# Gate/up remainders of three PSUM tiles behind one change to row tiles, in a fused attention and gated-MLP kernel

## The chip, the cores and the metric

The kernel runs on one NeuronCore of a Trainium2 chip. The metric is the device time of one execution in microseconds (us). Engines are named as in the profile: PE is TensorE's matmul side, PEld its weight loads, DVE is VectorE, ACT is ScalarE, POOL is GpSimd, SP is the SyncE queue that issues most DMAs.

## What is computed

One adaLN-conditioned transformer block on x of 2048 rows by 576 columns, in bf16. Attention is local and dilated (window 8, dilation 2, 32 heads of 18). The MLP is gated without a nonlinearity. Cut to what matters:

```python
mod = (silu(c) @ w_mod)                      # six rows of 576: sa, ca, ga, sb, cb, gb
h = layernorm(x) * (1 + ca) + sa
x = x + ga * attention(h, wqkv, wo)
h = layernorm(x) * (1 + cb) + sb
g = h @ w_gate                               # 576 -> 4608
u = h @ w_up                                 # 576 -> 4608
x = x + gb * ((g * u) @ w_down)              # 4608 -> 576
```

## The kernel before

**Tiling.** The 4608 hidden columns are 36 FF tiles of 128. The contraction over 576 is four full tiles of 128 rows and a remainder of 64. In `gate_up` a "main" step does the four full tiles for one FF tile, for gate (t=0) and up (t=1): 8 matmuls with 128 by 128 weights. The "remainder" does the last 64 rows. The gate's 64 weight rows lie in partitions 0 to 63 and the up's in 64 to 127 of one tile (`gr`), and the 64 remaining rows of h2T are held in both halves, so the two remainder matmuls use the two halves of the array's rows ("row tiles") and run side by side. One FF tile is thus 8 main matmuls and one pair of remainders.

**Passes.** The 2048 rows are cut into ten chunks (`SIZES`: four of 128, six of 256). Seven passes run gate/up: passes 0 to 3 on 128 rows each (the short passes, one chunk), passes 4 to 6 on 512 rows (the long passes, two chunks). After passes 3, 4, 5 and 6 a `down` stage multiplies the 512 rows gathered so far with w_down (L661). Each pass takes the FF tiles in nine blocks of four (`FB`), in an order that differs by pass (`ORDER`).

**Weights.** The main weights of a block (`gm`, 1 MB) and its remainder rows (`gr`, 128 KB) go through a ring of three buffers. Blocks 2 to 5 are kept during passes 0 to 3 in the place of w_down (so their matmuls show `wd` as input). `block_done` issues the next block's load, or in pass 3 the load of a part of w_down into a kept block's place; such a DMA starts once TensorE has read the old contents for the last time. All of these go through SP in the order in which they are written.

**PSUM.** `ps_mlp` has three tiles of two banks each, used by gate/up and by down; `ps_att` has two banks for the attention. A gate/up tile holds gate and up of one FF tile with 512 rows, or of two FF tiles with 128 rows. When it is complete, ScalarE copies it out as bf16 into one of two `gu` buffers (L644) and VectorE multiplies gate by up into `hh` (L645). These evacuations are traced under high priority.

**Order.** While a pass runs, the attention of the next pass's chunks is woven in: `project` makes q, k, v (L444, L451, L469); `attend` makes the logits (L512, with 32-column tiles of the array), the softmax, the weighted sum, the projection with wo (L583), the second layernorm and the transposes (L398) that give h2T for the next pass. They are generators. `step(ns)` in `gate_up` and `down` advances a Pacer's clock by so many ns of matmul time, and where the clock has come to the next part's share of the pass (`AT`, `AT_SHORT`; 0.60 for wo0, 0.80 for h2T in the short passes), the Pacer emits that part, one for each step. In passes 0 to 3 the framework's planner orders every engine by priority and by when it thinks that inputs are ready; in passes 4 to 6 TensorE runs in the order written, and the other engines are planned.

**Groups.** Remainders are gathered: in a short pass the two PSUM tiles of a block get their main matmuls and then their 8 remainders together; in a long pass two PSUM tiles are followed by their 4 remainders, twice in each block.

Of the kernel before, what the change touches and what calls it, by code (L numbers as in the profile page):

```python
# [7 lines left out]
BF = mybir.dt.bfloat16  # L8
F32 = mybir.dt.float32
ALU = mybir.AluOpType  # L10
# [7 lines left out]
P = 128  # L18
D = 576
DP = 640  # L20
KT = 5
# [10 lines left out]
CM = 512  # L32
# [4 lines left out]
FB = 4  # L37
AUTO = 4
GU_BUFS = 3
NB = FT // FB  # L40

ORDER = [[0, 1, 2, 3, 4, 5, 6, 7, 8], [6, 7, 8, 5, 4, 3, 2, 1, 0], [8, 1, 0, 5, 4, 3, 2, 6, 7],
         [2, 3, 4, 5, 0, 6, 7, 1, 8], [7, 1, 8, 0, 2, 3, 4, 5, 6], [4, 5, 6, 0, 1, 2, 3, 7, 8],
         [3, 7, 8, 0, 1, 2, 4, 5, 6]]
# [15 lines left out]
def kernel(  # L60
# [13 lines left out]
    nc = tc.nc  # L74
# [7 lines left out]
    def pool(name, bufs, **kw):  # L82
        return ctx.enter_context(tc.tile_pool(name=name, bufs=bufs, **kw))
# [13 lines left out]
    ps_mlp = pool("ps_mlp", 3, space=PSUM)  # L97
# [4 lines left out]
    def hp():  # L102
        return tc.high_priority()
# [11 lines left out]
    for sl, m0, off in ((slice(0, KT), 0, 0), (slice(KT, KT + 1), KT - 1, -64)):  # L115
        n = sl.stop - sl.start
# [132 lines left out]
    rows = {}  # L249
# [20 lines left out]
    gu_blocks = {}  # L270
# [45 lines left out]
    def load_next(ts=(0, 1)):  # L316
        if state["next"] < len(loads):
            load_gu(loads[state["next"]], ts)
            state["next"] += 1

    def load_wd(f0, f1):
        nc.sync.dma_start(wd[:, f0:f1, :], B_w_down[f0 * P:f1 * P, :].rearrange("(k p) n -> p k n", p=P))

    def block_done(pi, b):
        if pi == KEPT_PASSES - 1 and b in KEPT:
            k = KEPT.index(b)
            load_wd(k * WDB, (k + 1) * WDB)
        for n in range(len(loads)):
            if last_use[n] == (pi, b) and n + GU_BUFS == state["next"]:
                load_next()  # L330
# [16 lines left out]
    late = {}  # L347
# [246 lines left out]
    def gate_up(pi, c0, C, h2, step):  # L594

        hh = late["hh"]
        cs = slice(c0, c0 + C)  # L600
        ns = C / 2.4

        def main(out, gm, i, first):
            for t in range(2):
                for kt in range(KT - 1):
                    nc.tensor.matmul(out(t), lhsT=gm[:, kt, t, i * P:(i + 1) * P], rhs=h2[:, kt, cs],  # L606
                                     start=(kt == 0 and first), stop=False, skip_group_check=True)

        def rem(outs, gr, i):
            for hf in range(2):  # L610
                for t in range(2):
                    rows = slice(64 * t, 64 * (t + 1))
                    nc.tensor.matmul(outs[hf](t), lhsT=gr[rows, (i + 2 * hf) * P:(i + 2 * hf + 1) * P],  # L613
                                     rhs=h2[rows, KT - 1, cs], start=False, stop=True, skip_group_check=True)

        for b in ORDER[pi]:
            gm, gr = gu_blocks[b]
            todo = []
            for i in range(FB // 2):
                if C <= 256:  # L620

                    ps = ps_mlp.tile([P, 2, 2, 256], F32, name="pgu", tag="mlp")
                    outs = [lambda t, ps=ps, hf=hf: ps[:, t, hf, 0:C] for hf in range(2)]
                    evac = [(ps[:, :, :, 0:C].rearrange("p t n c -> p n t c"), slice(b * FB + i, b * FB + i + 3, 2))]
                else:
                    pss = [ps_mlp.tile([P, 2, 512], F32, name="pgu", tag="mlp") for _ in range(2)]
                    outs = [lambda t, ps=ps: ps[:, t, 0:C] for ps in pss]
                    evac = [(pss[hf][:, None, :, 0:C], slice(b * FB + i + 2 * hf, b * FB + i + 2 * hf + 1)) for hf in range(2)]
                todo.append((outs, i, evac))
                for hf in range(2):  # L630
                    main(outs[hf], gm, i + 2 * hf, hf == 0 or C > 256)
                    if hf == 0 or (C <= 256 and i == 0):
                        step(8 * ns)
                if C <= 256 and i == 0:
                    continue
                for outs, i, evac in todo:
                    rem(outs, gr, i)
                with hp():
                    for _, _, evac in todo:
                        for src, fs in evac:  # L640
                            n = src.shape[1]
                            gu = late["gup"].tile([P, 2 * CM], BF, name="gu")
                            g = gu[:].rearrange("p (n t c) -> p n t c", n=n, t=2)[:, :, :, 0:C]
                            nc.scalar.copy(g, src)  # L644
                            nc.vector.tensor_tensor(hh[:, fs, cs], g[:, :, 0, :], g[:, :, 1, :], ALU.mult)  # L645
                todo = []
                if i == FB // 2 - 1:
                    block_done(pi, b)
                step(10 * ns)

    def down(di, r0, x_t, step):
        to_load = [(cx, j) for cx in LOAD_X_DOWN.get(di, []) for j in range(SIZES[cx] // P)]
# [110 lines left out]
    def run_pass(pi):  # L763
        di, p = passes[pi]
        last = p is DOWN[di][-1]
        C = sum(SIZES[c] for c in p)
        total = FT * 9 * C / 2.4 + (FT * CM // P * 240 if last else 0)
        step = Pacer(passes[pi + 1][1] if pi + 1 < len(passes) else [], total)
        step(0)
        gate_up(pi, home[p[0]][1], C, h2T[di], step)  # L770
        if last:
            r0 = START[DOWN[di][0][0]]
            down(di, r0, [t for q in DOWN[di] for c in q for t in x_tiles[c]], step)
        step(0, rest=True)
# [36 lines left out]
```

## Time and profile before

| what | value |
|---|---|
| runs, median (lowest to highest) | 597.45 us (596.89 to 598.4), 4 runs |
| profiled execution | 596.89 us, span 595.1 us |
| granted TensorE clock | 1.0 |
| passes 0 to 3 with their attention | 38.7 to 161.8 us of the span |
| pass 4, pass 5, pass 6 (gate/up) | 216.2 to 306.9, 353.0 to 441.2, 481.0 to 553.8 us |
| casts of one gate/up tile on ScalarE | 587 ns (short), 1013 ns (long) |
| HBM read, written | 70.93 MB, 4.74 MB |

Between the passes lie the down stages. In the profile a group is named by its line, its engine and operation, and output<-inputs with their shapes; "x" counts instructions. In a timeline the first number is the start in us from the span's start, the second the duration of the merged piece. Ends of matmuls are modelled, so distances between starts say more than durations.

### The profile page before, as it was taken

The page shows a single profiled execution, that of the slowest core. Times are in us where ns is not written, and L with a number is a line of the kernel's source. Part 1 is how long each engine was busy: PE and PEld are TensorE (multiplying, and loading weights), DVE is VectorE, ACT ScalarE, POOL GpSimd, SP SyncE. Part 2 cuts the span into 40 slices and gives each one's busy share as a digit, 9 for nine tenths or more (in the row PEclk, how much of TensorE's full clock was granted, in tenths as well). Part 3 has the DMA queues.
Part 4 walks back from the last instruction along what each step waited for, and adds up shares of the span by engine and source line. Part 5 has one row for each costly group of instructions (what it writes and reads, how often), then busy time and mean ns, then how long its engine had stood idle before and what let it go on. Part 6 is the DMA issues. An engine that isn't in the chain of part 4 may idle for free.

```text
span 595.1 us, 12426 instructions
## 1 busy us (share of the span) xinstructions
PE 574.8 (97%) x5254; PEld 373.0 (63%) x5289; DVE 317.1 (53%) x705; ACT 261.5 (44%) x462; POOL 59.3 (10%) x117
## 2 busy tenths in 40 slices
PE   6879999999999999999999999999999999999996
PEld 3649798888878864544358874544458753433675
DVE  4767676767868766636385245834464422212101
ACT  3336667666552355456551145555540134444200
POOL 3530101010111200010001200011000000000000
PEclk9999999999999999999999999999999999999999
DMA  9999753459641333357000502456200004440000
GB/s 279 286 341 343 249 161 107 146 180 308 203 155 36 112 108 123 117 178 237 4 1 30 189 21 80 142 171 196 70 1 11 21 24 146 160 159 1 1 21 20
DMA packets 55073, 76.47 MB, mean 128 GB/s; under 512 B 3690, under 2 KB 48378, under 8 KB 55018
## 3 DMA queue, kind: packets, MB, share of 16 engines
q1 hardware_dynamic: 44922, 44.88, 24.4%
q0 software_dynamic: 7200, 27.48, 13.9%
q10 hardware_dynamic: 2896, 3.32, 1.6%
q8 instruction: 41, 0.67, 0.5%
q14 instruction: 14, 0.11, 0.1%
HBM read 70.93 MB, written 4.74 MB: 127 GB/s over the span
## 4 chain that ended last, share of the span: by engine, by line
PE 84%; DMA 6%; ACT 4%; DVE 4%; issue 1%; POOL 1%; ACTq 0%; SPq 0%; POOLq 0%; DVEq 0%
PE pgu L606 39%; PE acc L661 22%; PE pgu L613 6%; PE pq L444 5%; DMA wm<-in_w_mod_dram 3%; PE lgT L512 2%; PE pvA L469 2%; PE pvB L469 2%; DMA gm<-in_B_w_up_dram 1%; DMA wqk<-in_A_wqkv_dram 1%; PE pwB L583 1%; PE pwA L583 1%; PE turnA L398 1%; ACT gu L644 1%; ACT xn L377 1%
## 5 line engine op out<-in xcount | busy, mean ns | idle before, releaser
L606 PE MATMUL pgu<-h2T,gm 128*128 128x512 bf16 (+1 forms) x1473 | 238.1, 310 | 4.2 <-DMA wd<-in_B_w_gate_dram 1.5
L644 ACT CAST gu<-pgu 128x1024 bf16<-128x1024 f32 (+1 forms) x180 | 142.5, 844 | 137.1 <-PE pgu L613 127.4
L606 PEld LDWEIGHTS <-gm 128*128 128x128 bf16 x1504 | 117.7, 98 | 107.2 <-issue 17.6
L661 PE MATMUL acc<-wd,hh 128*128 128x288 bf16 x1152 | 147.4, 286 | 0.6 <-DVE y L667 0.6
L645 DVE TENSOR_TENSOR hh<-gu 128x512 bf16<-128x512 bf16 (+1 forms) x180 | 65.2, 368 | 145.8 <-ACT gu L644 145.0
L661 PEld LDWEIGHTS <-hh 128*128 128x128 bf16 x1152 | 111.8, 98 | 29.9 <-issue 2.4
L503 DVE TENSOR_TENSOR prod<-qT,kT 128x1280 bf16<-128x1280 bf16 (+1 forms) x80 | 46.3, 631 | 6.0 <-PE lgT L512 4.2
L613 PE MATMUL pgu<-h2T,gr 64*128 64x512 bf16 (+1 forms) x376 | 41.7, 312 | 0.9
L444 PE MATMUL pq<-hT,wqk 128*128 128x256 bf16 (+1 forms) x400 | 40.9, 251 | 1.6 <-DVE hT L408 1.6
L667 DVE TENSOR_TENSOR y<-acc,gb_bc 128x576 bf16<-128x576 f32 (+1 forms) x17 | 12.2, 715 | 54.3 <-PE acc L661 54.3
L570 DVE TENSOR_TENSOR vsh<-vsh,attn 128x2304 bf16<-128x2304 bf16 x30 | 39.8, 1350 | 0.7 <-DMA vsh<-vd 0.6
L486 POOL DMA_DIRECT2D vsh<-vd x30 | 22.4, 752 | 167.5 <-DMA vd<-v_sb 139.8
L444 PEld LDWEIGHTS <-wqk 128*128 128x128 bf16 x400 | 31.8, 98 | 8.9 <-issue 3.3
L606 PE MATMUL pgu<-h2T,wd 128*128 128x128 bf16 x512 | 34.2, 219 | 0.2 <-ACT gu L644 0.2
L670 POOL DMA_DIRECT2D out_dram<-y x15 | 8.2, 550 | 250.9 <-DVE y L669 239.4
L606 PEld LDWEIGHTS <-wd 128*128 128x128 bf16 x512 | 30.3, 98 | 1.4 <-issue 0.8
L377 ACT ACTIVATE xn<-x_t,ln_nmr,ln_rstd 128x576 bf16<-128x576 bf16 x31 | 26.2, 864 | 6.0 <-DVE ln_nmr L375 4.1
L613 PEld LDWEIGHTS <-gr 64*128 64x128 bf16 x376 | 10.9, 94 | 25.5 <-issue 21.2
L363 DVE BATCH_NORM_STATS2 ln_stats<-x_t 128x6 f32<-128x288 bf16 x64 | 26.0, 446 | 0.8
L446 ACT CAST kT<-pq 128x512 bf16<-128x512 f32 (+1 forms) x18 | 9.2, 519 | 26.0 <-PE pq L444 18.9
L571 DVE TENSOR_TENSOR vsh<-vsh 128x2304 bf16<-128x2304 bf16 x15 | 20.3, 1350 | 0.1
L367 ACT ACTIVATE ln_rstd<-ln_rstd 128x2 f32<-128x2 f32 (+1 forms) x20 | 4.1, 205 | 36.7 <-DVE ln_rstd L366 36.5
(132 smaller groups left out, 472.7 us busy)
## 6 DMA issues: line engine op xcount, KB each, us to landing
vsh<-vd POOLq DMA_DIRECT2D x30, 576.0 KB, 5.9
gm<-in_B_w_gate_dram SPq DMA_DIRECT2D x29, 512.0 KB, 3.7
gm<-in_B_w_up_dram SPq DMA_DIRECT2D x27, 512.0 KB, 5.2
wd<-in_B_w_down_dram SPq DMA_DIRECT2D x4, 1152.0 KB, 7.0
out_dram<-y POOLq DMA_DIRECT2D x15, 144.0 KB, 2.0
wd<-in_B_w_gate_dram SPq DMA_DIRECT2D x4, 512.0 KB, 18.1
wd<-in_B_w_up_dram POOLq DMA_DIRECT2D x4, 512.0 KB, 13.0
gr<-in_B_w_gate_dram SPq DMA_DIRECT2D x29, 64.0 KB, 4.9
```

Source lines behind the costliest of these rows:

```text
L363: nc.vector.bn_stats(stats[:, j, hf, :], src[j][:, hf * 288:(hf + 1) * 288])
L377: nc.scalar.activation(xn[:, j0 + j, 0:D], src[j][:], ACTF.Identity, bias=nmr[:, j:j + 1], scale=rstd[:, j:j + 1])
L444: nc.tensor.matmul(pq[:, gi, 0:C], lhsT=wqk[:, kt, w0:w0 + P], rhs=h[:, kt, :], start=(kt == 0), stop=(kt == KT - 1))
L469: nc.tensor.matmul(pv[q][:, 0:288], lhsT=h[:, kt, j * P:(j + 1) * P], rhs=wv[:, kt, q * 288:(q + 1) * 288], start=(kt == 0), stop=(kt == K ...
L486: nc.gpsimd.dma_start(vsh[:].rearrange("p w d h -> p w (d h)"), src)
L503: nc.vector.tensor_tensor(prod[:, 0:nm, 0:C], qT[:, 0:nm, 0:C], kT[:, 0:nm, off:off + C], ALU.mult)
L570: nc.vector.tensor_tensor(vsh[:], vsh[:], attn[:, j, ws, None, :].to_broadcast([P, WG, DH, H]), ALU.mult)
L606: nc.tensor.matmul(out(t), lhsT=gm[:, kt, t, i * P:(i + 1) * P], rhs=h2[:, kt, cs], start=(kt == 0 and first), stop=False, skip_group_chec ...
L613: nc.tensor.matmul(outs[hf](t), lhsT=gr[rows, (i + 2 * hf) * P:(i + 2 * hf + 1) * P], rhs=h2[rows, KT - 1, cs], start=False, stop=True, sk ...
L644: nc.scalar.copy(g, src)
L645: nc.vector.tensor_tensor(hh[:, fs, cs], g[:, :, 0, :], g[:, :, 1, :], ALU.mult)
L661: nc.tensor.matmul(acc[:, q, 0:288], lhsT=hh[:, f, j * P:(j + 1) * P], rhs=wd[:, f, q * 288:(q + 1) * 288], start=(f == 0), stop=(f == FT ...
```

## The change

Tiles are now numbered through the whole pass ("units": two neighbouring FF tiles in a short pass, one in a long pass) and taken three at a time. Main of the first and of the second; then the remainders of all three, which close the first two tiles and open the third; then a step of the Pacer, the evacuations of the first two, main of the third, which closes it, and its evacuation. `block_done` is called after the group in which a block ended. In a short pass `step` now follows each main; before, the second main of a block's last tile had none. The steps' times add up to 54 units of C/2.4 ns for six FF tiles in every pass; before it was 34 for the four FF tiles of a block in a short pass and 36 in a long one.

```diff
-        def main(out, gm, i, first):
-            for t in range(2):
-                for kt in range(KT - 1):
-                    nc.tensor.matmul(out(t), lhsT=gm[:, kt, t, i * P:(i + 1) * P], rhs=h2[:, kt, cs],
-                                     start=(kt == 0 and first), stop=False, skip_group_check=True)
-
-        def rem(outs, gr, i):
-            for hf in range(2):
...
-        for b in ORDER[pi]:
-            gm, gr = gu_blocks[b]
-            todo = []
-            for i in range(FB // 2):
...
-                todo.append((outs, i, evac))
-                for hf in range(2):
-                    main(outs[hf], gm, i + 2 * hf, hf == 0 or C > 256)
-                    if hf == 0 or (C <= 256 and i == 0):
-                        step(8 * ns)
-                if C <= 256 and i == 0:
-                    continue
-                for outs, i, evac in todo:
-                    rem(outs, gr, i)
-                with hp():
...
-                            nc.scalar.copy(g, src)
-                            nc.vector.tensor_tensor(hh[:, fs, cs], g[:, :, 0, :], g[:, :, 1, :], ALU.mult)
-                todo = []
-                if i == FB // 2 - 1:
-                    block_done(pi, b)
-                step(10 * ns)
+        nf = 2 if C <= 256 else 1
+        units = [(b, i) for b in ORDER[pi] for i in range(0, FB, nf)]
+
+        def main(u, first):
+            (b, i), out = units[u], ps[u]
+            for n in range(nf):
+                for t in range(2):
+                    for kt in range(KT - 1):
+                        nc.tensor.matmul(out[:, t, n, 0:C], lhsT=gu_blocks[b][0][:, kt, t, (i + n) * P:(i + n + 1) * P], rhs=h2[:, kt, cs],
+                                         start=(first and n == 0 and kt == 0), stop=(not first and kt == KT - 2), skip_group_check=True)
+                step(8 * ns)
+
+        def rem(u, first):
...
+                    nc.tensor.matmul(out[:, t, n, 0:C], lhsT=gu_blocks[b][1][rows, (i + n) * P:(i + n + 1) * P], rhs=h2[rows, KT - 1, cs],
+                                     start=(first and n == 0), stop=not first, skip_group_check=True)
+
+        def evacuate(u):
...
+                nc.scalar.copy(g, ps[u][:, :, :, 0:C].rearrange("p t n c -> p n t c"))
+                nc.vector.tensor_tensor(hh[:, fs, cs], g[:, :, 0, :], g[:, :, 1, :], ALU.mult)
+
+        ps, done = {}, 0
+        for u in range(0, len(units), 3):
+            for k in range(3):
+                ps[u + k] = ps_mlp.tile([P, 2, nf, 512 // nf], F32, name="pgu", tag="mlp")
+                if k < 2:
+                    main(u + k, True)
+            for k in range(3):
+                rem(u + k, k == 2)
+            step(6 * nf * ns / 2)
+            evacuate(u)
+            evacuate(u + 1)
+            main(u + 2, False)
+            evacuate(u + 2)
+            while done < NB and (done + 1) * FB <= (u + 3) * nf:
+                block_done(pi, ORDER[pi][done])
+                done += 1
```

More of the change, by code (lines that the diff above doesn't have):

```diff
@@ new lines, in main @@
+        def main(u, first):
[7 more added lines that the diff above has]
+        def rem(u, first):
+            (b, i), out = units[u], ps[u]
+            for n in range(nf):
@@ L611, in rem @@
                 for t in range(2):
                     rows = slice(64 * t, 64 * (t + 1))
-                    nc.tensor.matmul(outs[hf](t), lhsT=gr[rows, (i + 2 * hf) * P:(i + 2 * hf + 1) * P],
-                                     rhs=h2[rows, KT - 1, cs], start=False, stop=True, skip_group_check=True)
-        for b in ORDER[pi]:
-            gm, gr = gu_blocks[b]
-            todo = []
-            for i in range(FB // 2):
[L620 to L628, printed above, removed]
-                todo.append((outs, i, evac))
-                for hf in range(2):
-                    main(outs[hf], gm, i + 2 * hf, hf == 0 or C > 256)
-                    if hf == 0 or (C <= 256 and i == 0):
-                        step(8 * ns)
-                if C <= 256 and i == 0:
-                    continue
-                for outs, i, evac in todo:
-                    rem(outs, gr, i)
-                with hp():
[L639 to L643, printed above, removed]
-                            nc.scalar.copy(g, src)
-                            nc.vector.tensor_tensor(hh[:, fs, cs], g[:, :, 0, :], g[:, :, 1, :], ALU.mult)
-                todo = []
-                if i == FB // 2 - 1:
-                    block_done(pi, b)
-                step(10 * ns)
@@ new lines, in rem @@
+                    nc.tensor.matmul(out[:, t, n, 0:C], lhsT=gu_blocks[b][1][rows, (i + n) * P:(i + n + 1) * P], rhs=h2[rows, KT - 1, cs],
+                                     start=(first and n == 0), stop=not first, skip_group_check=True)
+        def evacuate(u):
+            b, i = units[u]
+            fs = slice(b * FB + i, b * FB + i + nf)
+            with hp():
+                g = late["gup"].tile([P, 2 * CM], BF, name="gu")[:, 0:2 * nf * C].rearrange("p (n t c) -> p n t c", n=nf, t=2)
+                nc.scalar.copy(g, ps[u][:, :, :, 0:C].rearrange("p t n c -> p n t c"))
+                nc.vector.tensor_tensor(hh[:, fs, cs], g[:, :, 0, :], g[:, :, 1, :], ALU.mult)
```

## The prediction

> **What bounds the kernel now.** I read the page's busy times first, then its slices.
>
> ```profile
> span 595.1 us, 12426 instructions
> PE 574.8 (97%) x5254; PEld 373.0 (63%) x5289; DVE 317.1 (53%) x705; ACT 261.5 (44%) x462; POOL 59.3 (10%) x117
> ...
> PE   6879999999999999999999999999999999999996
> ```
>
> TensorE is busy for 97% of the span, and after the first three slices hardly rests; no other engine passes 53%. The granted clock is full in every slice. So time is gained only where TensorE does less or waits less. A busy TensorE is not one at its peak, so I looked next at how its matmuls follow each other, in the timeline of TensorE in the last long pass, which no attention work interrupts:
>
> ```profile
> 485.20 3.63 PE L606 MATMUL pgu<-h2T,gm 128*128 128x512 bf16 x16
> 488.76 0.60 PE L613 MATMUL pgu<-h2T,gr 64*128 64x512 bf16 x4
> 489.29 3.63 PE L606 MATMUL pgu<-h2T,gm 128*128 128x512 bf16 x15
> ```
>
> and in the chain that ended last, which gives the bare rates:
>
> ```profile
> 123.79 1.79 PE pgu L606 x32
> ...
> 233.08 1.73 PE pgu L606 x8
> ```
>
> 1.73/8 is 0.216 us for a 512-column matmul, 1.79/32 is 0.056 us for a 128-column one. From 485.20 to 489.29 one period of the long pass takes 4.09 us. It holds 16 main matmuls and two pairs of remainders, whose halves (64 rows each) start 3 to 4 ns apart: 18 slots of 0.216, 3.89 us. Some 0.20 us are left. The start times show where: from the last main matmul to the first remainder 311 ns, from the last remainder to the next main matmul 308 ns, against 216. That is 95 ns to change to row tiles and 92 ns to change back. With 128 columns the same two distances are 152 and 148 against 56: the same price, so it doesn't scale with the matmul. A round trip costs 0.187 us, and nothing covers it, since TensorE itself stands.
>
> The third reading is the TensorE timeline at the end of the first short pass, which shows what else holds it:
>
> ```profile
> 62.12 1.95 PE L606 MATMUL pgu<-h2T,gm 128*128 128x128 bf16 x32
> 64.00 0.40 PE L613 MATMUL pgu<-h2T,gr 64*128 64x128 bf16 x8
> 64.33 0.40 PE L606 MATMUL pgu<-h2T,gm 128*128 128x128 bf16 x4
> 65.51 1.74 PE L606 MATMUL pgu<-h2T,gm 128*128 128x128 bf16 x28 [0.79 <-DMA gm<-in_B_w_up_dram]
> 67.18 0.23 PE L613 MATMUL pgu<-h2T,gr 64*128 64x128 bf16 x2
> 67.34 0.34 PE L398 MATMUL turnA<-identw,xn 128*128 128x128 bf16 x3
> ...
> 68.86 1.74 PE L606 MATMUL pgu<-h2T,gm 128*128 128x128 bf16 x28 [0.25 <-DMA gm<-in_B_w_up_dram]
> ```
>
> Two things. Blocks 7 and 8 wait for their weights, so the end of pass 0 is pinned to an arrival (the chain has the same transfer as "60.06 8.75 DMA"). And a transpose of the attention sits inside a remainder group, which makes three round trips of one; passes 1 and 2 show the same at 95.24 and 127.73. The last view is the table of windows in pass 3:
>
> ```profile
> 148.00:152.00 4.00, 4.00 (x64) 3.66 (x62) 4.00 (x6) 1.84 (x5) 0.00 (x0) 1.00 1.09 351
> 152.00:156.00 4.00, 4.00 (x61) 3.62 (x59) 3.97 (x7) 2.34 (x6) 0.00 (x0) 1.00 1.08 309
> ```
>
> The last two columns are DMA share and GB/s. The DMA engines are full from 136 to 156: four loads of w_down (issued at 134.23, 137.23, 140.51, 143.80, each as a kept block is released), then blocks 1 and 8. Block 1's up half lands at 154.74, its remainder rows at 155.13 and 155.32, and TensorE starts block 1 at 155.2. There is no slack.
>
> **The change part by part.** *Fewer changes.* A short pass has 9 remainder groups now and gets 6 (18 tiles of two FF tiles, three to a group); a long pass 18, and gets 12. Four short passes: 36 to 24. Three long: 54 to 36. The count of matmuls stays. Long passes: 18 round trips at 0.187 are 3.37 us, all on the path, because TensorE there waits for nothing (its largest stall in 216 to 554 is 0.57 us, one projection waiting for hT). Short passes: 12 at 0.187 are 2.24 us, 0.56 a pass. Passes 1 and 2 keep theirs: 1.12 us.
>
> *Pass 0.* Its 0.56 us goes into the wait for block 8, whose arrival doesn't move: the DMA engines are full there too (share 1.07 from 40.2 to 64.5), and its issue waits for queue space, not for the release of block 1, which comes one tile (0.9 us) later in the new order. From the gate on, 28 main matmuls were left with 8 remainders; now the same with 12, two slots of 0.056: +0.1 us. Bounds: -0.56 (if arrivals move too) and +1.0 (if block 7's remainder rows, landing at 65.66 and just after, hold the third tile's remainders, which now come before its main).
>
> *Pass 3.* Two edits hurt. The second kept block is released with the second group, one tile later, so the second w_down load issues about 1 us later; the first still flows until about 140, so up to 1 us of transfer time may be lost. And block 1 (tiles 14, 15) needs its remainder rows before the main of tile 14, so at about 154.4 instead of 158.6, while they land at 155.3. After that moment remains what remained before. So the 0.56 us is lost and a little more: I take +0.3, between -0.56 (arrivals move with the pass) and +1.5 (both delays in full). I lean to the lower half because the queue, once full, delivers at the same rate.
>
> *Split groups.* Each transpose inside a group costs two extra round trips, 0.37 us. In the new order the attention is emitted slightly earlier in the pass (a block's paces add to 54 per six FF tiles, where they added to 34 per four), so the transposes fall elsewhere; remainders hold only about a fifth of the pass. In passes 1 and 2 that gives up to 0.75 us; it may also stay as it is. I take half, -0.37.
>
> *The third tile's remainder waits for an empty tile.* This is the added wait. There are three PSUM tiles, and all three are now held at a change. What is queued behind is the rest of TensorE's stream. Two main stages pass between the end of the earlier third tile and this wait: about 3.5 us long, 1.8 us short. The cast that must end by then takes 1013 ns (128x1024) or 587 ns (128x512), and may start 1.73 or 0.9 us after the previous group, behind two casts that by then are all but done. That leaves about 2 us and 0.9 us, more than one attention activation of the row xn (864 ns). The first tile of the next group has one main stage of cover, as now, and the trace shows what that costs: two stalls of about 0.4 us in 36 short blocks. So 0, with an upper bound of 24 waits of 0.1 us, 2.4 us; below nothing, at most 0.8, since those two stalls could go.
>
> The Trainium skill, TensorEngine Tiling (Array Packing), under Restrictions and Gotchas, says that row tiling raises PSUM pressure, and under Performance Considerations that the copy out of PSUM may become the bound. That speaks against holding all three tiles at once. Read at its worst, one cast waited for in each group, it would make 36 x 1.013 + 24 x 0.587 = 50.6 us of loss; by the rows above it is nothing, and no run here shows it yet.
>
> *Weight loads.* In the long passes a block comes free up to one tile later (2 us); its successor is needed two blocks (17 us) after issue and lands in 4 to 7, so this stays hidden at no cost. If that cover were gone, it would be 2 us for each load. The step ahead of the evacuations emits attention work a moment earlier; evacuations keep their priority: nothing.
>
> Sum: -3.37 - 1.12 + 0.1 + 0.3 - 0.37 = -4.46. The profiled execution took 596.89 us (span 595.1 and 1.8 around it), so 592.4; the median of the runs, 597.45, is 0.56 above it, so 593.0.
>
> **The rivals.** *The short passes give nothing* because their planned order splits the larger groups as often as before, or the two pinned passes lose in full: then only the long passes count, 3.37 less about 0.5 to 1.5, giving 594.6 to 595.5. For it: three of the four short passes are split now, two are pinned. Against it: only 3 of the 36 groups are split now.
>
> *Slower: the transposes come too early.* Place: the last attention step of short passes 0 to 2, where the projection with wo ends (91.14 in pass 1) and xn is ready only at 95.9, 4.7 us later, by a chain of VectorE and ScalarE that the change doesn't shorten. Between stand about 4.2 us of gate/up work, and TensorE already stalls about 0.5 us there. If the new order put the transposes right behind wo, each pass would lose up to 4.2 us, some 8 to 12 us in all, less 4.5: 601 to 605. It decides from 1.5 us more per pass, when less than about 2.7 us, five FF tiles at 0.56, is left between. The paces plan 0.2 of 36 tiles, 7.2, so I give it little.
>
> *More than reckoned.* Arrivals move with the passes, the splits and both PSUM stalls go: -5.6 - 0.75 - 0.8, about 590.3.
>
> **How the numbers follow.** Forecast (592 to 594) 0.5; short passes give nothing (594.6 to 595.5, some of it to 596.2) 0.26; more than reckoned 0.08; slower 0.10; and 0.06 for savings that small waits eat up wholly. A measurement here can tell about 0.2% (1.2 us) from no change: faster 0.84, same 0.06, slower 0.10. The range, 590.8 to 596.5, leaves out the slower case and the far end of the best.
>
> **What would show it.** Right: in the last pass a period of three FF tiles takes 6.0 us (27 slots and one round trip) with x6 at L613's place and 60 changes in all where unsplit; pass 6's gate/up shortens by 1.1 to 1.2 us; passes 0 and 3 end no earlier, relative to their starts; TensorE waits for remainder rows (gr) in pass 3. Wrong: if a change costs more with six or twelve remainders behind it, if ScalarE's cast ends TensorE's waits in most groups, or if a short pass grows by over 1 us.

## The result and the profile after

The changed kernel takes 597.79 us (median of 37 runs) against 597.76 us for the kernel before (59 runs): a ratio of 1.0003, interval 0.9994 to 1.0012. That is no change, where 593.0 was forecast. The profiled execution took 597.87 us, span 596.1.

The page after, first its span, busy times and TensorE's slices:

```profile
span 596.1 us, 12425 instructions
PE 570.1 (96%) x5254; PEld 376.6 (63%) x5289; DVE 318.0 (53%) x705; ACT 263.5 (44%) x462; POOL 60.7 (10%) x117
...
PE   6878899999999999999999999999999999999996
```

TensorE is busy for 4.7 us less and the span is no shorter: the work went, and idle time came. The timeline of TensorE in the last pass shows that the work went as planned:

```profile
487.62 5.35 PE L612 MATMUL pgu<-h2T,gm 128*128 128x512 bf16 x24
492.90 0.82 PE L621 MATMUL pgu<-h2T,gr 64*128 64x512 bf16 x6
493.66 5.35 PE L612 MATMUL pgu<-h2T,gm 128*128 128x512 bf16 x23
```

One period of three FF tiles takes 6.04 us, 27 slots of 0.216 and 0.21 for one round trip. In the whole trace TensorE changes its tiling 176 times against 248 before. 60 of the 72 are the 30 round trips; the other 12 are the transposes that no longer split a group.

The idle time shows in the table of waits (engine and line, who it waited for, us in total, times, longest), here TensorE's own waits from 38 to 222 us, which covers the short passes and the first down stage. Before:

```profile
PE pgu L606 <- DMA wd<-in_B_w_gate_dram: 1.5, 1, 1.5
PE pgu L606 <- DMA gm<-in_B_w_up_dram: 1.0, 2, 0.8
PE turnA L398 <- ACT xn L377: 0.9, 2, 0.4
PE pgu L606 <- ACT gu L644: 0.5, 2, 0.2
```

and after:

```profile
PE pvB L469 <- ACT kT L454: 3.2, 3, 2.5
PE turnA L398 <- ACT xn L377: 2.0, 3, 0.7
PE pgu L612 <- DVE h2T L408: 1.5, 1, 1.5
PE pgu L621 <- DMA gr<-in_B_w_gate_dram: 1.5, 1, 1.5
PE turnB L398 <- ACT xn L379: 0.7, 3, 0.2
PE turnB L398 <- DVE dd L532: 0.4, 2, 0.2
```

A wait of 1.5 us for the first matmul of pass 0 is in both tables, at L606 before and at L612 after. Before, 2.4 us of other waits are left; after, 7.8 us in these lines and 0.7 in smaller ones. By stage, from the start of the first main weight load of each pass (us; the forecast of -0.37 for the splits is shared between passes 1 and 2):

| stage | before | after | difference | forecast |
|---|---|---|---|---|
| start of pass 0 | 38.66 | 39.08 | +0.4 | 0 |
| pass 0 | 32.19 | 34.91 | +2.7 | +0.1 |
| pass 1 | 28.14 | 28.71 | +0.6 | -0.75 |
| pass 2 | 32.49 | 32.58 | +0.1 | -0.75 |
| pass 3 and down | 84.71 | 86.58 | +1.9 | +0.3 |
| from pass 4 to the end | 378.92 | 374.21 | -4.7 | -3.37 |

Three new waits carry the short passes' loss. **The first** is in passes 0 to 2, at the v projection. TensorE's timeline in pass 0:

```profile
57.90 0.40 PE L469 MATMUL pvA<-wv,hT 128*128 128x288 bf16 x2 [0.16 <-ACT kT L446]
60.82 0.41 PE L469 MATMUL pvB<-wv,hT 128*128 128x288 bf16 x2 [2.52 <-ACT kT L454]
```

pvB needs an attention bank that ScalarE's copy L454 empties. The copy takes 0.26 us, so what matters is what it stands behind. ScalarE's timeline:

```profile
56.98 0.58 ACT L629 CAST gu<-pgu 128x512 bf16<-128x512 f32 x1 [1.13 <-DVE hh L630]
57.47 0.38 ACT L446 CAST kT<-pq 128x256 bf16<-128x256 f32 x1
59.74 0.58 ACT L629 CAST gu<-pgu 128x512 bf16<-128x512 f32 x1 [1.90 <-DVE hh L630]
60.22 0.26 ACT L452 CAST qT<-pr 64x128 bf16<-64x128 f32 x1
60.50 0.26 ACT L454 CAST kT<-pr 64x128 bf16<-64x128 f32 x1
```

It stands behind a gate/up cast that waits 1.90 us for VectorE to free one of the two gu buffers. VectorE's timeline in that time:

```profile
56.81 1.35 DVE L571 TENSOR_TENSOR vsh<-vsh 128x2304 bf16<-128x2304 bf16 x1
58.20 0.76 DVE L572 TENSOR_TENSOR vsh<-vsh 128x1152 bf16<-128x1152 bf16 x1
58.99 0.46 DVE L573 TENSOR_TENSOR o_sb<-vsh 128x576 bf16<-128x576 bf16 x1
59.37 0.48 DVE L630 TENSOR_TENSOR hh<-gu 128x256 bf16<-128x256 bf16 x2
```

The multiplies that free the buffers (L630) stand behind 2.6 us of the attention's weighted sum. In the kernel before, ScalarE came to the same copy (56.76) with nothing of the kind ahead of it, and the next casts waited for no buffer:

```profile
56.48 0.26 ACT L452 CAST qT<-pr 64x128 bf16<-64x128 f32 x1 [0.80 <-PE pr L451]
56.76 0.26 ACT L454 CAST kT<-pr 64x128 bf16<-64x128 f32 x1
57.15 1.07 ACT L644 CAST gu<-pgu 128x512 bf16<-128x512 f32 x2
```

So, as read from these rows, one buffer too few holds ScalarE, ScalarE holds a bank, and the bank holds TensorE. The run with four buffers below tests it.

**The second** is at the transposes near the end of passes 0 to 2, in TensorE's timeline of pass 1:

```profile
98.40 0.34 PE L398 MATMUL turnA<-identw,xn 128*128 128x128 bf16 x3 [0.66 <-ACT xn L377]
...
99.69 0.23 PE L398 MATMUL turnB<-identw,xn 128*128 128x128 bf16 x1 [0.23 <-ACT xn L379]
```

By the start times they hold TensorE for 0.83 and 0.39 us in each of the three passes, where before it was 0.51 in two of them. **The third** is in pass 3, the remainder rows of block 1:

```profile
158.62 0.40 PE L621 MATMUL pgu<-h2T,gr 64*128 64x128 bf16 x8
160.47 0.51 PE L621 MATMUL pgu<-h2T,gr 64*128 64x128 bf16 x4 [1.46 <-DMA gr<-in_B_w_gate_dram]
```

Eight remainders run, and the four that open the third tile wait.

### The profile page after: what moved, and what is told of

It is laid out like the page before. It is cut to its first block, busy times and chain, and to the rows that moved or that the text cites. A ratio compares the mean times of both kernels' runs of the same rounds, so it can differ in the third digit from the quotient of the medians.

```text
span 596.1 us, 12425 instructions
## 1 busy us (share of the span) xinstructions
PE 570.1 (96%) x5254; PEld 376.6 (63%) x5289; DVE 318.0 (53%) x705; ACT 263.5 (44%) x462; POOL 60.7 (10%) x117
## 4 chain that ended last, share of the span: by engine, by line
PE 82%; DMA 6%; DVE 6%; ACT 3%; issue 2%; ACTq 0%; POOL 0%; POOLq 0%; DVEq 0%
PE pgu L612 37%; PE acc L660 23%; PE pgu L621 6%; PE pq L444 5%; DMA vd<-v_sb 3%; PE lgT L512 2%; DMA vsh<-vd 2%; PE pwA L583 1%; PE pwB L583 1%; PE pvB L469 1%; PE pvA L469 1%; ACT gu L629 1%; DMA gr<-in_B_w_gate_dram 1%; PE turnA L398 1%; PE turnB L398 1%
## 5 line engine op out<-in xcount | busy, mean ns | idle before, releaser
L612 PE MATMUL pgu<-h2T,gm 128*128 128x512 bf16 (+1 forms) x1473 | 237.6, 311 | 3.9 <-DVE h2T L408 1.5
L629 ACT CAST gu<-pgu 128x1024 bf16<-128x1024 f32 (+1 forms) x180 | 145.3, 843 | 109.1 <-PE pgu L621 79.8
L612 PEld LDWEIGHTS <-gm 128*128 128x128 bf16 x1504 | 119.2, 98 | 106.1 <-issue 15.5
L630 DVE TENSOR_TENSOR hh<-gu 128x512 bf16<-128x512 bf16 (+1 forms) x180 | 65.6, 368 | 133.7 <-ACT gu L629 132.6
L621 PE MATMUL pgu<-h2T,gr 64*128 64x512 bf16 (+1 forms) x376 | 37.2, 311 | 1.5 <-DMA gr<-in_B_w_gate_dram 1.5
L612 PE MATMUL pgu<-h2T,wd 128*128 128x128 bf16 x512 | 34.0, 219 | 0.0
L612 PEld LDWEIGHTS <-wd 128*128 128x128 bf16 x512 | 30.3, 98 | 1.0 <-issue 0.2
L621 PEld LDWEIGHTS <-gr 64*128 64x128 bf16 x376 | 12.3, 94 | 20.7 <-issue 11.7
L469 PEld LDWEIGHTS <-hT 128*128 128x128 bf16 x160 | 15.2, 98 | 9.0 <-issue 4.9
```

What stands on the lines that cost most here:

```text
L469: nc.tensor.matmul(pv[q][:, 0:288], lhsT=h[:, kt, j * P:(j + 1) * P], rhs=wv[:, kt, q * 288:(q + 1) * 288], start=(kt == 0), stop=(kt == K ...
L612: nc.tensor.matmul(out[:, t, n, 0:C], lhsT=gu_blocks[b][0][:, kt, t, (i + n) * P:(i + n + 1) * P], rhs=h2[:, kt, cs], start=(first and n = ...
L621: nc.tensor.matmul(out[:, t, n, 0:C], lhsT=gu_blocks[b][1][rows, (i + n) * P:(i + n + 1) * P], rhs=h2[rows, KT - 1, cs], start=(first and ...
L629: nc.scalar.copy(g, ps[u][:, :, :, 0:C].rearrange("p t n c -> p n t c"))
```

## The experiments

My theory after the result: the long passes keep what was forecast, and the short passes give theirs back in these three waits. The rivals: a round trip costs less than reckoned, or TensorE's waits are only pushed from place to place, so that taking one away gains nothing.

**New grouping in the long passes alone.** Both versions of `gate_up` stand in the kernel:

```diff
+    def gate_up(pi, c0, C, h2, step):
+        (gate_up_new if C > 256 else gate_up_old)(pi, c0, C, h2, step)
```

> New grouping in the long passes alone, the short ones as before. My theory (the long passes keep their savings, the short ones give theirs back and more in new waits): 18 round trips at 0.187 us and the lost 0.57 us wait, 3.5 to 4.5 us faster than before, about 593.5; the start of pass 4 stays near 216 us of the span. Rival (a change costs less than reckoned, or what is saved comes back as waits in the long passes too): within 1 us of before.

Measured: 593.76 us against 597.59, ratio 0.9941 (0.9927 to 0.9956). Pass 4 starts at 216.45 us, as expected, and from there to the end it takes 374.4 us against 378.9. The long passes' gain is real and stands alone.

**New grouping in the short passes alone.** The same with `C <= 256`.

> New grouping in the short passes alone, the long ones as before. My theory: 2 to 6 us slower than before, with pass 4 starting about 5 us later, as after the whole change. Rival (the short passes' new order costs nothing itself, and the profiled execution after the change only caught an accidental half-clock window): 1 to 3 us faster, as forecast for them.

Measured: 602.8 us, ratio 1.0088 (1.0071 to 1.0104). The short passes lose 5.2 us, and the two halves (-3.8 and +5.2) add up to the whole within 1.4 us. The rival falls as far as it promised a gain. A half-clock window (a stretch of about 3.4 us in which TensorE's granted clock is half; rows in the last section) is in it, though: the profiled execution has a second one at 161.2, and five of the six runs list the same mean granted clock of 0.994. It may make up the 1.4 us that are left over; that is not shown.

**Four gu buffers in the short passes**, each of half the size; the last two lines stand ahead of pass 4.

```diff
-        late["gup"] = pool("gup", 2)
+        late["guard"] = tc.tile_pool(name="gups", bufs=4)
+        late["gup"] = late["guard"].__enter__()
...
-                g = late["gup"].tile([P, 2 * CM], BF, name="gu")[:, 0:2 * nf * C]
+                g = late["gup"].tile([P, CM if C <= 256 else 2 * CM], BF, name="gu")[:, 0:2 * nf * C]
...
+    late["guard"].__exit__(None, None, None)
+    late["gup"] = pool("gup", 2)
```

> The whole change, with four gu buffers of half the size in the short passes instead of two (one tile there needs only half a buffer); nearly the same instruction order on every engine. Theory (the third cast of a group waits for VectorE to free a gu buffer, and ScalarE's copies of q, k, v stand behind it, so TensorE waits for an attention bank at pvB): the waits at pvB in passes 0, 1 and 2 (2.7, 0.7 and 0.3 us) go, 2.5 to 4 us faster than the changed kernel. Rival (TensorE's wait is for the data of the attention, and ScalarE's wait is only its image): less than 1 us.

Measured: 595.63 us, ratio 0.997 (0.9959 to 0.9982), 2.0 us under the kernel before in the same session and 2.2 under the changed kernel's median, somewhat less than expected. The traces have the same order of instructions on every engine, but for one instruction of VectorE that moves by one place; so it is the buffers. TensorE's timeline shows the wait gone at its place in pass 0 (429 ns between the starts of pvA's second and pvB's first matmul, where it was 2.80 us):

```profile
58.33 0.41 PE L470 MATMUL pvA<-wv,hT 128*128 128x288 bf16 x2
58.88 0.41 PE L470 MATMUL pvB<-wv,hT 128*128 128x288 bf16 x2
```

and, later in the same pass, where a part of the gain went:

```profile
66.02 0.40 PE L622 MATMUL pgu<-h2T,gr 64*128 64x128 bf16 x8
67.14 0.48 PE L622 MATMUL pgu<-h2T,gr 64*128 64x128 bf16 x4 [0.72 <-DMA gr<-in_B_w_gate_dram]
```

TensorE now comes to block 7 before its remainder rows do. Before the repair this wait did not show: the longer one came ahead of it.

**The transposes later.**

```diff
-AT_SHORT = dict(AT, oT=.55, wo0=.60, h2T=.80)
+AT_SHORT = dict(AT, oT=.55, wo0=.60, h2T=.88)
```

> The whole change, with the share of the pass at which the last transposes of a short pass are emitted moved from 0.80 to 0.88; they then stand 24 main matmuls (1.3 us) later on TensorE. Theory (they now come ahead of xn, for 0.83 and 0.39 us in each of passes 0 to 2): most of 3.6 us goes, 2 to 3.6 us faster than the changed kernel. Rival (the waits move to the start of the next pass, which then waits for h2T): within 1 us.

Measured: 597.31 us, ratio 0.9988 (0.9972 to 1.0003): by the time the rival, though the waits that came are not for h2T. The waits at the transposes are gone, but in each of passes 0 to 2 a main matmul now waits 0.85 us for a PSUM tile, and at the start of passes 2 and 3 another 0.40 us; both end with ScalarE's cast. The kernel below, which has the same transposes, shows why.

**Pass 3 grouped as before**, the rest changed (`pi != 3` as the condition).

> The whole change, but pass 3 grouped as before. Theory (in pass 3 the third tile's remainders come one main stage before the block's weights would be needed, and the second w_down load is released later; both lie on a full DMA stretch, so TensorE waits 1.6 us for remainder rows): that wait goes, pass 3 and its down stage fall from 86.6 us back to 84.7, and the half-clock window that sometimes follows the wait becomes rare; 2 to 3 us faster than the changed kernel, 595 to 596. Rival (the transfers end when they end, so TensorE waits as long at another place of pass 3): within 0.7 us of the changed kernel.

Measured: 595.79 us, ratio 0.9967 (0.9952 to 0.9981), 2.0 us under the changed kernel's median. Pass 3 and its down stage take 84.52 us, and TensorE no longer waits for remainder rows. So the transfers do arrive in time for the old order. The new order asks for them one main stage earlier and also starts them later (the next section has the times); this run undoes both and does not part them. Half-clock windows became rarer too, as expected: 2 of the 11 runs list a mean granted clock of 0.994 or less, where 20 of the 37 of the changed kernel do.

**Both repairs together**, four gu buffers and 0.88.

> The whole change with both repairs, four gu buffers in the short passes and the transposes at 0.88. If the two waits are separate, the gains add: 2.0 and 0.5 us, so about 595.2, and pass 1 takes 28.0 us. If the wait of 0.85 us that took the transposes' place in the run with 0.88 (a main matmul waiting for ScalarE) was itself for want of gu buffers, it goes too: up to 2.5 us more, 593 to 594. If both repairs ran into the same arrival of weights in pass 0, less than the sum: 595.5 to 596.5.

Measured: 596.17 us, ratio 0.9964 (0.9949 to 0.9979), not better than the buffers alone. Pass 1 takes 27.92 us, as expected. Pass 0 takes 32.97, since TensorE waits 1.78 us for block 7's remainder rows at 64.48 and then 0.74 us for block 8. The third of the expected answers holds: both repairs ran into the same arrivals. With `gate_up` as before in that pass, pass 0 ended at 70.9, 71.1 and 71.2 us in three kernels that entered it at 38.7, 37.5 and 37.9, and at 72.2 in a fourth that entered at 38.9: the first three ends are closer together than their starts, which speaks for an arrival that sets them; the fourth does not fit.

**Mixed**: new grouping in the long passes and in passes 1 and 2, there with both repairs; passes 0 and 3 as before.

```diff
+        (gate_up_new if pi not in (0, 3) else gate_up_old)(pi, c0, C, h2, step)
...
-        at = AT_SHORT if SIZES[ci] == P else AT
+        at = dict(AT_SHORT, h2T=.88) if ci in (2, 3) else AT_SHORT if SIZES[ci] == P else AT
```

> New grouping in the long passes and in passes 1 and 2, there with four gu buffers and the transposes at 0.88; passes 0 and 3, which end on arrivals of weights, as before. Theory: the long passes' gain stays whole, and passes 1 and 2 give a part of their 0.94 us each: 592.5 to 593.5, the fastest of all. Rival (the planned order of any short pass eats what the changes save): not faster than the kernel with new grouping in the long passes alone, 593.8.

Measured: 593.32 us, ratio 0.9922 (0.9908 to 0.9935), faster than both kernels, as expected. The runs do not tell it apart from new grouping in the long passes alone (593.76), so the rival is not ruled out; the traces show passes 1 and 2 shorter by 0.27 and 0.08 us. What takes the rest of their 0.94 us is in TensorE's timeline

```profile
94.90 1.07 PE L670 MATMUL pgu<-h2T,gm 128*128 128x128 bf16 x16
96.65 1.05 PE L670 MATMUL pgu<-h2T,gm 128*128 128x128 bf16 x16 [0.69 <-ACT gu L687]
```

and in ScalarE's:

```profile
94.83 0.20 ACT L369 ACTIVATE ln_rstd<-ln_rstd 128x1 f32<-128x1 f32 x1
95.27 0.87 ACT L378 ACTIVATE xn<-x_t,ln_nmr,ln_rstd 128x576 bf16<-128x576 bf16 x1 [0.23 <-DVE ln_nmr L376]
96.04 1.05 ACT L687 CAST gu<-pgu 128x512 bf16<-128x512 f32 x2
```

The remainders that close two tiles end at 94.9, but their casts stand behind the layernorm's chain on ScalarE until 96.04, and the next tile's main waits for the first of them. The planner had put xn ahead.

**Groups of one in the long passes**: each tile's two remainders follow its main; short passes as before.

```diff
+        for u in range(len(units)):
+            ps[u] = ps_mlp.tile([P, 2, nf, 512 // nf], F32, name="pgu", tag="mlp")
+            main(u, True)
+            rem(u, False)
+            step(2 * nf * ns / 2)
+            evacuate(u)
...
```

> The price of a round trip by itself: short passes as before, and in the long passes each tile's pair of remainders follows its main matmuls, so 108 groups in place of 54 in the three passes. At 0.187 us a round trip, on the path in full: 54 more cost 10.1 us, about 607.7. Rival (a part of the price belongs to a group's weight loads or is hidden by its neighbours, so that it isn't linear in the number of groups): under 605 or over 611.

Measured: 607.9 us, ratio 1.0173 (1.0154 to 1.0193). From pass 4 to the end the trace has 389.2 us, 10.26 more than before for 54 more round trips: 0.190 us each. The timeline of the last pass gives the same, 2.16 us for 9 slots of 0.216 and one trip:

```profile
492.09 1.90 PE L669 MATMUL pgu<-h2T,gm 128*128 128x512 bf16 x8
493.92 0.39 PE L678 MATMUL pgu<-h2T,gr 64*128 64x512 bf16 x2
494.24 1.90 PE L669 MATMUL pgu<-h2T,gm 128*128 128x512 bf16 x8
```

The price is linear in the number of groups, from one pair a group to three.

## Why the prediction was wrong

**The price of a change and the long passes: right.** 0.187 us was read from distances of starts, and the groups of one confirmed it. The term of 3.37 us was small rather than large: 4.5 to 4.7 us in the traces, 3.8 in the medians. The wait of 0.57 us in pass 4 went too; what the rest is, no run settles.

**The added wait of the third tile: the step that failed.** From pass 0 to the first down stage the sum had a gain of 1.1 us, and the traces show a loss of 5.7. The sum put this term at 0, by comparing when the cast "must end" with the stages that TensorE needs. That looked at PSUM tiles and TensorE alone. The wait that came is one resource further: a third cast in a group needs a third gu buffer, there are two, and the one whose turn it is is freed by a multiply behind 2.6 us of attention on VectorE. The step "evacuations keep their priority: nothing" hid this: priority did not put those multiplies ahead of the weighted sum in the order that the planner made. With four buffers about 2 us came back, so about that much is shown for this term; its upper bound was 2.4 us, set for another reason, and the sum took 0. The casts behind xn, of 0.85 us, are the wait that the step did describe, in the form in which it appears once the transposes move.

**The split groups: right in what goes, wrong in what comes.** All 12 changes of the splits went. The rival of transposes that come too early was right in its mechanism and place: TensorE waits 1.2 us at the transposes of each of passes 0 to 2, about 0.7 more than in passes 1 and 2 before. That is under the 1.5 us from which it would have decided by itself. Its price and the gain of -0.37 were kept apart as if only one could happen.

**Pass 3: the mechanism right, the size past the end of its bounds.** The wait for remainder rows is where it was put, and the stage lost 1.9 us where +0.3 was taken and +1.5 was the bound. Going to the lower half was the mistake: block 1's first load was issued 1.3 us later relative to the pass (at 151.86 instead of 146.78, the pass having started 3.8 us later), and its remainder rows were needed earlier as well. It began with the second w_down load, for which about 1 us of delay was reckoned. It was issued at 143.24 instead of 137.23, 2.2 us later relative to the pass.

**Pass 0: pinned, as said, but the new waits reach beyond the pin.** The saving went nowhere, as forecast. The two waits of 2.7 and 1.2 us, and in the profiled execution a half-clock window at 41.7, then carried the pass past the arrival of its weights: the trace of the changed kernel has no wait for them there. How much of the 2.7 us that the pass lost belongs to the window is not shown. The bound of +1.0 did name the remainder rows of block 7; they showed as soon as the wait at pvB was gone.

**The copies out of PSUM.** The Trainium skill, TensorEngine Tiling (Array Packing), Performance Considerations, says that after a fourfold speedup of TensorE the copy out of PSUM may become the bottleneck. The prediction weighed that against rows of cast durations and put it aside. Here the copies do hold TensorE at a few places of the short passes: 3.2 us at pvB in the table of waits, or 0.85 and 0.40 us at a time once the transposes move, and not the 50.6 of the worst reading. They do so because of what they queue behind, not because of how long they take: ScalarE is busy for 44% of the span.

## What to carry to other kernels

A saving on the busiest engine is only worth what the stage around it can take: sum it by stage, and for each stage name the arrival or the buffer that is late next. Where a change makes work come in bursts (three copies instead of two), count every buffer along the way, not the first one alone, and ask on each in-order engine what stands ahead of the instruction that frees it. A stage that is ordered by a planner can change sign with the grouping; undoing the change there alone kept 3.8 us here.

## What the runs showed of the hardware

After some waits TensorE's granted clock falls to half for a window of about 3.4 us. In the kernel with pass 3 grouped as before, the table of windows (the number ahead of the last two columns is the granted clock) has, around the wait of 2.5 us at 57.9 to 60.4:

```profile
58.00:62.00 4.00, 1.60 (x15) 1.40 (x15) 3.32 (x11) 1.54 (x5) 0.00 (x0) 0.92 1.09 305
62.00:66.00 4.00, 4.00 (x45) 3.53 (x44) 0.54 (x2) 1.91 (x5) 0.55 (x1) 0.65 1.11 312
```

and in the kernel with new grouping in the short passes alone, after a wait of 1.7 us for remainder rows at 160.4:

```profile
160.00:164.00 4.00, 3.58 (x25) 2.66 (x26) 3.44 (x8) 0.70 (x2) 0.00 (x0) 0.65 0.52 153
164.00:168.00 4.00, 4.00 (x61) 3.65 (x59) 0.29 (x1) 1.29 (x3) 1.49 (x2) 0.92 0.25 73
```

TensorE's timeline there shows the half: the matmuls of the v projection start 0.12 us apart, and inside the window 0.24.

```profile
160.41 0.48 PE L678 MATMUL pgu<-h2T,gr 64*128 64x128 bf16 x4 [1.74 <-DMA gr<-in_B_w_gate_dram]
...
161.08 0.29 PE L469 MATMUL pvA<-wv,hT 128*128 128x288 bf16 x1
161.20 0.40 PE L469 MATMUL pvB<-wv,hT 128*128 128x288 bf16 x1
...
162.12 0.44 PE L469 MATMUL pvB<-wv,hT 128*128 128x288 bf16 x1
162.36 0.44 PE L469 MATMUL pvA<-wv,hT 128*128 128x288 bf16 x1
```

In either pair of rows 0.08 and 0.35 of 4 us are missing from the full clock, 1.7 us in all; at half the clock that is a window of 3.4 us. In the second kernel the stage took 87.95 us against 86.58 in the profile of the changed kernel, whose clock stayed full at that place. Of these 1.4 us, 0.3 are the longer wait (1.74 instead of 1.46). Not every wait of this length is followed by such a window: the profile of the changed kernel has none after the same two waits, and one at 41.7, behind the wait of 1.5 us at the start of pass 0.

The windows are more frequent after the change. A mean granted clock of 0.994 goes with two of them in the profile of the second kernel above, and 0.996 with one in that of the changed kernel. Of the changed kernel's 37 runs 20 list 0.994 or less (median 598.9 us), and 14 list 0.996 or more (597.5); of the 42 runs of the kernel before that were taken beside the experiments, 4 list 0.994 or less. So a part of what the short passes lost is clock and not wait. It doesn't decide the result: the 14 runs are no faster than the kernel before either.

The Trainium skill, TensorE: Matmul & The Clock Gate, Part 1, gives the half clock after at least one idle window of about 3.4 us, and the full clock after a busy one of about that length. The second agrees with the 3.4 us of these rows; the idle time ahead of them was shorter here, 2.5 and 1.7 us.
